# A hand-planned attention and mixer kernel: the steps of its first fifty microseconds in another order, two more q/k groups transposed whole-array

## The chip, the cores and the metric

The kernel runs on one core of one Trainium2 chip. The metric is the device time of one execution in microseconds (us). Three runs of the kernel before gave 184.23, 184.74 and 185.72 us, so the median is 184.74 us.

Engines are named as in the profile: PE is TensorE, ACT is ScalarE, DVE is VectorE, POOL is GpSimd, and SP is SyncE, which here issues nearly all DMAs.

## What is computed

Sigmoid attention for 8 batches of 12 heads, 448 rows and 64 columns each, followed by a token mixer and an output product. In short, from the reference:

```python
scores = scale * np.matmul(q, k.transpose(0, 1, 3, 2)) - np.log(S)
attn = 1.0 / (1.0 + np.exp(-scores))
x = np.matmul(attn, v)            # heads side by side: (8, 448, 768)
wq = x @ w_q                      # (8, 448, 64)
wk = x @ w_k
W_tok = scale * np.einsum('bsd,btd->bst', wq, wk)
mixed = np.einsum('bst,btd->bsd', W_tok, x)
out = np.maximum(mixed, 0.0) @ w_out
```

## The kernel before

The work is cut into 24 groups of four heads (three groups to a batch). A group has seven slices of keys. For each slice PE makes the scores (step S: four 64-column matmuls that use the four quarters of the array at once), ACT takes the sigmoid (line 332, one instruction of 128x896 for each S), and PE multiplies by v (step P, accumulating over the seven slices). After a group's seventh P the result is copied out of the accumulator as `xt` (line 356). Over the whole run that makes 168 S, 168 sigmoids and 168 P.

Before its S steps a group needs q and k transposed. They come in as f32 by DMA, are cast to bf16 on POOL or DVE (lines 212 and 222), and are then transposed in one of these ways, chosen by a letter in the plan:

- `q` with `k` or `j`: on PE in 64x64 pieces, 28 matmuls for q and 28 for k, then one copy of both by DVE (line 301; for group 1 two copies at line 293).
- `a` with `b`: on PE with the whole array, seven 128x128 matmuls each, into a single accumulator bank, each followed by its own DVE copy (line 280).
- `r` with `s` and `z`, or `c` with `d`: on DVE by 32x32 stream transposes (lines 265, 252 and 272), without PE.

The mixer's steps are x (transposing `xt` into `xn`: `x` by 28 pieces of 64x64, `X` by seven whole-array matmuls), W (the products with w_q and w_k, whole-array in this part), N, U and M (the mixer itself), and O (half an output chunk; whole-array in this part; `o` means that ACT copies the finished chunk out, `O` that DVE does). E and F are matmuls of zeros.

**What sets the order.** Nothing is scheduled by the compiler. A string `PLAN` of 669 letters is walked from left to right, and each letter issues one step on all the engines that it uses. Every engine runs its own instructions strictly in that order. A second string, `BANKS`, gives each step in turn its part of the accumulator memory (digits are pairs of banks, letters are single banks): a step waits until the step that had this part before has been read out. So S steps wait for earlier sigmoids through `BANKS`, and whether a copy runs on DVE or ACT is a matter of upper or lower case (`P` or `p` at a group's seventh slice).

Loads go through a ring of six f32 buffers in the order of the string `ORDER`. SP issues a load only when the buffer's former content has been cast, and SP is a queue too, so a late cast holds up all loads behind it. `BEHIND` makes single loads wait for a numbered matmul, and `HELD` does the same for three stores. `1` casts the next load of a short list on DVE (v of group 0, k of group 2). `D` sends finished output tiles on their way if there are any.

In the words below, S8 is the eighth S and "sigmoid 8" its sigmoid; a stretch of whole-array work is a run of steps that use PE as one 128-wide array, between steps that use its quarters.

Of the kernel before, what the change touches and what calls it, by code (L numbers as in the profile page):

```python
# [17 lines left out]
def kernel(  # L18
# [29 lines left out]
    def pool(name, bufs, **kw):  # L48
# [15 lines left out]
    pairs = [banks[:, 2 * n : 2 * n + 2] for n in range(4)]  # L64
    pairs16 = [banks16[:, 2 * n : 2 * n + 2] for n in range(4)]
    BANKS = (
        "abcd0123200233111020302312031203101031021g2012020120h1g21320"
        "132123103103213012302g01h20h1g2031a32102312g12h1201321gh0210"
        "12h01210321g201321g2h01gh201g20132cd302c302302131e301230ef31"
        "0ef3102102c302d320d320123cd20gh120g102310g102hg102312gh10210"  # L70
        "ef130210ef1302120120320312321031021021321a310320321320120123"
        "020210320120c3210210312"
    )
    given = list("".join(BANKS))
    held = set()
# [54 lines left out]
    def xt(u, j):  # L130
# [5 lines left out]


    PLAN = (
        "SSFKESSES1EEqESDD1DESjPPppSpDpPDSSSqS1kSpPPSqSpSkSDPPSPSxSxr"
        "sSWwDDDDSSwzDPpSPppSpPSrSwSwWsSPpXSPNpSpPPSUSqSzMSSkpSpPpSMS"  # L140
        "ppPSSxSxMScPpSdPSpppSSPwWwrWSSXWDWSSosOSNPpPSpppzPSSOOSxSrPP"
        "ppSUSsppzPSoSOSoSoSppMpSPPPPSSWOWWWScSdxWODSMDWSOSxCOSMppScP"
        "DppSPPDSodDoSpxPDPDSCPrPSpDSPOOSNSsSOoDzOOSUSXcSPdpPSSpPPSPo"
        "OWSMSwowWMSSOwWCScpppSxpdpSpPSOoMSPPcDSPPpSpSPOoNSSSdDOoDOOp"
        "xDSPpPxSPpPDSuwcWwdSSMWOoSMSDwwOOSDxpPSPrPSmPpPDooNDSDSosoOz"
        "oSDDSxOOSUDpSDPPPDSPpcDSPoDODSSSodOoOSPMpSPPPSPPSwWwoScMSdOw"
        "wSSWOONSPMPcpSPPPPSSOodXSOSxoSoxSOppSpcUPSPpPSoOSdSxOOSPPPmp"
        "pPSPoSoMmOSOLScllLSLLSDodODSONxOPSpcpdpDPSPSPoOSoSOSOoSUSoSO"
        "SpPPpp1SoSOpSPOSOyppPMpPpplMlmlxlLlxOoONooUoOMmooOmooOoOOOOO"
        "oOOOOooOo"  # L150
    )
    PLAN = "".join(PLAN)
    KIND = ["a"] + [t for t in PLAN if t in "qacr"]
# [364 lines left out]

    opened = []
    stores, o_tiles = [], [0]  # L520
    HELD = {(5, 1, 1): 3040, (5, 2, 0): 3168, (5, 2, 1): 3168}

    def flush(n=None):

# [45 lines left out]
    def out_pair(act, tail):  # L570
# [36 lines left out]
        def store():  # L607
            for x in range(2):
                cols = slice(x * NB, (x + 1) * NB)
                if len(us) == 1:  # L610
                    behind_product(
                        (nc.scalar if ends and x else nc.sync).dma_start(
                            out=out[2 * w + us[0]].rearrange("(p i) d -> p i d", i=NI)[:, k : k + 5 : 4, cols], in_=o[HALF[x]],
                        ), HELD.get((2 * w + us[0], k, x), 0),
                    )
# [6 lines left out]

        stores.append((o_tiles[0] - 1, max(HELD.get((2 * w + us[0], k, x), 0) for x in range(2)), store))
        if tail or late:
# [74 lines left out]
    for _ in range(31):  # L699
# [2 lines left out]

    ORDER = (
# [5 lines left out]
    )  # L709
    BEHIND = {("q", 23): (2280, 2280), ("v", 23): (2816, 2530)}  # L710
    BY = {"s": [], "v": []}
    for x in ORDER.split():
        if x[0] == ".":
# [10 lines left out]
    def pump_loads():  # L724
        while len(loaded) < len(ORDER):
            nm, n = ORDER[len(loaded)]
            if len(ring) >= 6 and ring[-6] not in cast:
                break
            emit, m = BEHIND.get((nm, n), (0, 0))
            if emit >= len(products):  # L730
# [204 lines left out]
```

## Time and profile before

| | before |
|---|---|
| median of three runs | 184.74 us |
| profiled execution, its time | 184.71 us |
| its span, first to last instruction | 182.8 us |
| outside the span (184.71 - 182.8) | 1.9 us |
| sigmoids | 168, busy 141.1 us |
| stores and loads | 48.51 MB, mean 265 GB/s |

The profile comes from one execution, which has a time of its own beside its span; the two differ by what lies around the instructions. The page gives for each engine the share of the span in which it was busy. Busy ends of matmuls are modelled and include the time until the last column is out, so PE can read as busy while no new matmul starts; where this matters the start times of successive matmuls are used instead. A group's row gives its count, total, mean length and the idle time in front of it with what ended that. In the timeline, rows with a count merge instructions of the same kind, and the bracket behind a row is the idle time ahead of it.

### The profile page before, as it was taken

How to read it: one execution, taken by the hardware profiler on the slowest of the kernel's cores; microseconds unless marked ns; L12 is line 12 of the kernel's file. 1: busy time of each engine (PE TensorE's matmuls, PEld its weight loads, DVE VectorE, ACT ScalarE, POOL GpSimd, SP SyncE). 2: the span in 40 equal slices, each digit the busy share in tenths (PEclk: the TensorE clock that was granted, in tenths of full speed). 3: DMA queues.
4: the chain of work that ended last, by engine and by line, in shares of the span. 5: the costliest groups of instructions: out<-in, count | busy, mean ns of one | idle time of the engine just before them, and what ended most of it. 6: DMA issues, size and time to landing. Idle time of an engine off the chain costs nothing.

```text
span 182.8 us, 8404 instructions
## 1 busy us (share of the span) xinstructions
PE 170.4 (93%) x3617; PEld 112.8 (62%) x3618; DVE 134.3 (73%) x205; ACT 159.4 (87%) x207; POOL 116.8 (64%) x156
## 2 busy tenths in 40 slices
PE   7887789899999999999999999999999999999980
PEld 7644435545564555565556556556788798899960
DVE  2545699988998898988858887689786885694220
ACT  4699999999999999999998999899989979966230
POOL 1336886999589999699999927999999500000000
PEclk9999999999999999999999999999999999999997
DMA  5999999969999677999999999997589343433775
GB/s 174 371 382 274 329 382 398 364 212 279 351 402 331 219 295 207 353 285 349 396 232 327 349 307 292 359 359 250 193 255 252 106 96 87 95 90 93 176 181 164
DMA packets 24261, 48.51 MB, mean 265 GB/s; under 512 B 3872, under 2 KB 16416, under 8 KB 24224
## 3 DMA queue, kind: packets, MB, share of 16 engines
q1 hardware_dynamic: 24000, 47.69, 79.4%
q8 instruction: 28, 0.46, 1.0%
q10 hardware_dynamic: 224, 0.30, 0.7%
q14 instruction: 9, 0.07, 0.1%
HBM read 35.78 MB, written 11.01 MB: 256 GB/s over the span
## 4 chain that ended last, share of the span: by engine, by line
PE 76%; ACT 12%; DMA 3%; POOL 3%; issue 2%; DVE 1%; POOLq 0%; ACTq 0%
PE banks L121 72%; ACT at L332 12%; PE banks L124 4%; DMA ld<-in_v_dram 3%; POOL v L222 1%; POOL qk L212 1%; POOL qk L173 1%; POOL wout L755 0%; DVE xn L385 0%; ACT qk L806 0%; DVE ld L558 0%; ACT ld L558 0%; DVE zeros L691 0%; DVE zeros L690 0%; POOLq L222 0%
## 5 line engine op out<-in xcount | busy, mean ns | idle before, releaser
L332 ACT ACTIVATE at<-banks 128x896 bf16<-128x896 f32 x168 | 141.1, 943 | 5.4 <-PE banks L121 4.8
L121 PE MATMUL banks<-wout,mx 64*64 64x384 bf16 (+2 forms) x816 | 65.4, 324 | 0.0
L121 PE MATMUL banks<-qk 64*64 64x448 bf16 x672 | 60.7, 360 | 3.8 <-ACT at L332 3.0
L212 POOL CAST qk<-ld 128x896 bf16<-128x896 f32 x38 | 44.7, 1191 | 8.2 <-issue 5.6
L121 PEld LDWEIGHTS <-mx 64*64 64x64 bf16 (+2 forms) x816 | 39.2, 105 | 16.2 <-issue 6.0
L121 PE MATMUL banks<-at,v 64*64 64x448 bf16 x672 | 46.5, 350 | 0.8 <-ACT at L332 0.4
L121 PEld LDWEIGHTS <-qk 64*64 64x64 bf16 x672 | 26.5, 105 | 24.8 <-issue 17.8
L356 DVE CAST xt<-banks 128x896 bf16<-128x896 f32 x23 | 25.0, 1086 | 7.6 <-PE banks L121 5.7
L121 PEld LDWEIGHTS <-v 64*64 64x64 bf16 x672 | 22.9, 106 | 6.8 <-issue 1.7
L470 DVE TENSOR_SCALAR mx<-banks 128x896 bf16<-128x896 f32 (+1 forms) x21 | 19.9, 956 | 4.9 <-PE banks L121 4.2
L222 POOL CAST v<-ld 128x896 bf16<-128x896 f32 x22 | 20.3, 930 | 2.9 <-DMA ld<-in_v_dram 2.7
L272 DVE STREAM_TRANSPOSE qk<-qk 128x448 f32<-128x448 f32 x26 | 16.0, 630 | 0.1
L385 DVE COPY xn<-banks 128x896 bf16<-128x896 bf16 x21 | 13.1, 624 | 3.6 <-PE banks L124 2.6
L252 DVE STREAM_TRANSPOSE qk<-qk 32x448 f32<-32x448 f32 x24 | 15.3, 636 | 0.6
L170 POOL COPY qk<-qk 32x448 uint32<-32x448 uint32 x26 | 14.4, 554 | 1.6
L173 POOL COPY qk<-swap 32x448 uint32<-32x448 uint32 x26 | 14.4, 554 | 1.5
L121 PE MATMUL banks<-xt,wqk 64*64 64x448 bf16 (+1 forms) x84 | 13.8, 353 | 0.2 <-ACT at L332 0.2
L651 DVE COPY o<-banks 128x384 f32<-128x384 f32 x17 | 9.4, 554 | 3.4 <-PE banks L121 3.0
L124 PEld LDWEIGHTS <-xt 64*64 64x64 bf16 (+1 forms) x588 | 9.8, 108 | 3.0 <-issue 1.5
L124 PE MATMUL banks<-ident,xt 64*64 64x64 bf16 (+1 forms) x588 | 10.4, 194 | 0.2
L121 PE MATMUL banks<-wqk,tmp 64*64 64x448 bf16 (+3 forms) x72 | 8.5, 291 | 0.0
L121 PE MATMUL banks<-wq,tmp 64*64 64x448 bf16 (+2 forms) x72 | 8.4, 292 | 0.0
(67 smaller groups left out, 135.3 us busy)
## 6 DMA issues: line engine op xcount, KB each, us to landing
ld<-in_q_dram SPq DMA_DIRECT2D x24, 448.0 KB, 6.2
ld<-in_v_dram SPq DMA_DIRECT2D x24, 448.0 KB, 5.9
ld<-in_k_dram SPq DMA_DIRECT2D x23, 448.0 KB, 5.9
out_dram<-o SPq DMA_DIRECT2D x38, 192.0 KB, 4.7
out_dram<-ld SPq DMA_DIRECT2D x14, 192.0 KB, 2.8
ld<-in_moe_w_out_dram SPq DMA_DIRECT2D x6, 384.0 KB, 4.6
wout<-wout SPq DMA_DIRECT2D x6, 192.0 KB, 6.0
out_dram<-o SPq DMA_DIRECT2D x4, 96.0 KB, 1.9
```

What stands on the lines that cost most here:

```text
L121: products.append(nc.tensor.matmul(*args, **kw))
L124: products.append(nc.tensor.transpose(*args, **kw))
L170: eng.tensor_copy(out=w[lo, 1], in_=w[hi, 0])
L173: eng.tensor_copy(out=w[hi, 0], in_=z[lo])
L212: COPY[e](out=f[:, :, "qk".index(nm)].rearrange("p e i d y -> p e y i d"), in_=ld.pop((nm, n)).rearrange("p (y i e d) -> p e y i d", y=2, ...
L222: COPY[e](out=t16.rearrange("p i b d -> p b i d"), in_=ld.pop((nm, n)).rearrange("p b (i d) -> p b i d", i=NI),)
L252: nc.vector.transpose(out=qk[n][other : other + 32, h].rearrange("p t i n -> p (t i n)").bitcast(F32), in_=w[own : own + 32, 1 - h],)
L272: nc.vector.transpose(out=qk[n][:, t].rearrange("p t i n -> p (t i n)").bitcast(F32), in_=w)
L332: nc.scalar.activation(dst, src, ACTF.Sigmoid, bias=attn_bias, scale=attn_scale)
L356: COPY[eng](out=xt(u, j), in_=ps)
L385: COPY[eng](out=xn, in_=ps)
L470: nc.vector.tensor_scalar(dst, ps, moe_scale, 0.0, ALU.mult, ALU.max)
```

## The change

The strings `PLAN` and `BANKS` are others, `HELD` has other matmul numbers, and `BEHIND` loses its entry for q of group 23 and has other numbers for v of group 23. `ORDER` is only broken into lines at other places: the loads stand in the same order. The last 340 letters of `PLAN` are the same in both. Of the two strings one line each is shown, at the place where `PLAN` begins:

```diff
     PLAN = (
-        "SSFKESSES1EEqESDD1DESjPPppSpDpPDSSSqS1kSpPPSqSpSkSDPPSPSxSxr"
...
+        "SSFKESSES1EEDDqESDSjSSDS1pDPPpSpSPqpp1kSPpPpSSapSPSSbSxSSXSS"
...
-    HELD = {(5, 1, 1): 3040, (5, 2, 0): 3168, (5, 2, 1): 3168}
+    HELD = {(5, 1, 1): 2916, (5, 2, 0): 3044, (5, 2, 1): 3044}
...
-    BEHIND = {("q", 23): (2280, 2280), ("v", 23): (2816, 2530)}
+    BEHIND = {("v", 23): (2746, 2404)}
```

Counted over the strings, up to the 340 letters that both share: the number of S, P, W, O, N, U, M, E and x steps is the same. Group 3 goes from `q`,`k` to `a`,`b`; group 4 goes from `r`,`s`,`z` to `a`,`b`. Two of the x steps (of groups 1 and 3) go from `x` to `X`. The `xt` copies of groups 0 and 2 go from DVE to ACT. Two more output chunks are copied by ACT and two fewer by DVE. One pair of S steps shares one sigmoid instruction of 128x1792. The kernel issues 70 matmuls fewer in all. Counted in stretches of whole-array work, there are six before S48 and twenty from there to S97 in the kernel before; in the changed kernel there are nine and eighteen.

On ACT, from its first sigmoid on, one piece of the difference (`at` is the sigmoid's output, `xt` a group's result, `o` an output chunk):

```order
-L332 ACTIVATE at<-banks 128x896 x63
+L332 ACTIVATE at<-banks 128x896 x12
+L356 CAST xt_90<-banks 128x2x7x64
+L332 ACTIVATE at<-banks 128x896 x14
+L356 CAST xt_92<-banks 128x2x7x64
+L332 ACTIVATE at<-banks 128x896 x37
 L651 COPY o<-banks 128x384
```

The 63 sigmoids that stood in a row now have two copies of 128x896 among them, after the twelfth and after the twenty-sixth.

On DVE, the rows from the first cast of a whole load to the copies of x, in the kernel before (`q_233` is q of group 1, `v_286` v of group 0, `k_413` k of group 2, `qk_453` the cast q and k of group 4):

```order
L222 CAST q_233<-ld_102 128x2x7x64
L293 COPY qk<-banks 128x2x448
L222 CAST v_286<-ld_104 128x2x7x64
L293 COPY qk<-banks 128x2x448
L356 CAST xt_90<-banks 128x2x7x64
L222 CAST k_413<-ld_105 128x2x7x64
L301 COPY qk<-banks 128x2x2x448 x2
L356 CAST xt_91<-banks 128x2x7x64
L385 COPY xn<-banks 128x896 x2
L265 STREAM_TRANSPOSE qk<-qk_453 128x448 x2
L252 STREAM_TRANSPOSE qk<-qk_453 32x448 x4
```

And the same place of the changed kernel:

```order
L222 CAST q_233<-ld_102 128x2x7x64
L293 COPY qk<-banks 128x2x448 x2
L222 CAST v_335<-ld_104 128x2x7x64
L222 CAST k_413<-ld_105 128x2x7x64
L301 COPY qk<-banks 128x2x2x448
L280 COPY qk<-banks 128x7x2x64
L356 CAST xt_91<-banks 128x2x7x64
L280 COPY qk<-banks 128x7x2x64
L385 COPY xn<-banks 128x896 x2
L280 COPY qk<-banks 128x7x2x64 x2
```

The cast of k of group 2 no longer stands behind a copy of `xt`, both copies of group 1's q and k come ahead of the cast of v, and six stream transposes have given way to copies at line 280.

On PE, around S71 of the kernel before (`wqk` with `xt` is a W step, `wout` with `mx` an O step, `qk` an S step, the `wq`,`tmp` matmul the end of an M step):

```order
L121 MATMUL banks<-wq_99,tmp 64x448
L121 LDWEIGHTS wqk_84
L121 MATMUL banks<-xt_92,wqk_84 128x448
L121 LDWEIGHTS qk
L121 MATMUL banks<-qk 64x448
...
L121 LDWEIGHTS mx
L121 MATMUL banks<-wout_83,mx 128x384
```

And of the changed kernel:

```order
L121 MATMUL banks<-wq_99,tmp 64x448
L121 LDWEIGHTS qk
L121 MATMUL banks<-qk 64x448
...
L121 LDWEIGHTS wqk_84
L121 MATMUL banks<-xt_92,wqk_84 128x448
L121 LDWEIGHTS mx
L121 MATMUL banks<-wout_83,mx 128x384
```

The W step now stands right ahead of the O step, so that the two make one stretch of whole-array work. At S62 and S63 two O steps come together in the same way.

More of the change, by code (lines that the diff above doesn't have):

```diff
@@ L66 @@
     BANKS = (
[L67 to L72, printed above, removed]
+        "abcd230010132022211321302312301g010h1230e31ef03e10033e01f320"
+        "32023102310310g213201302g01h20h1g2031a32102312g121h021301gh0"
+        "21012h01210321g201321gh201gh201g20132cd302c302302131f301230e"
+        "f310ef3102102c302d320d320123cd20gh120g102310g102hg102312gh10"
+        "210ef130210ef1302120120320312321031021021321a310320321320120"
+        "123020210320120c3210213212"
     )
@@ L138 @@
     PLAN = (
-        "SSFKESSES1EEqESDD1DESjPPppSpDpPDSSSqS1kSpPPSqSpSkSDPPSPSxSxr"
[L140 to L150, printed above, removed]
+        "SSFKESSES1EEDDqESDSjSSDS1pDPPpSpSPqpp1kSPpPpSSapSPSSbSxSSXSS"
+        "awwDSSbpPrSppPppwDWSESwWXDSPNSPDPpSpSDspPUSSzSMSqkPDSPSPMPSp"
+        "pPSSXxSSSMpppcSdPppSPSwDwDrWwSSXWWSsCSOOSDDNPzpSpppSpSPoOSxS"
+        "rppPPSUSsPpPzSOSOSDSOoSPMPSpPPSPPSWowwcSSdxOWWSCMSWODSxoSMpP"
+        "SPPpSpcPSOdoSPxrpSpPpSPPDSOoNSTSszOoOOSUSXScppSPpppSdSPOOWSM"
+        "SDwWoWMSSwWOScPpCpSxPppSDdPDSOoMSPPcDSPPpSpSPOoNSSSdDOoDOOpx"
+        "DSPpPxSPpPDSuwcWwdSSMWOoSMSDwwOOSDxpPSPrPSmPpPDooNDSDSosoOzo"
+        "SDDSxOOSUDpSDPPPDSPpcDSPoDODSSSodOoOSPMpSPPPSPPSwWwoScMSdOww"
+        "SSWOONSPMPcpSPPPPSSOodXSOSxoSoxSOppSpcUPSPpPSoOSdSxOOSPPPmpp"
+        "PSPoSoMmOSOLScllLSLLSDodODSONxOPSpcpdpDPSPSPoOSoSOSOoSUSoSOS"
+        "pPPpp1SoSOpSPOSOyppPMpPpplMlmlxlLlxOoONooUoOMmooOmooOoOOOOOo"
+        "OOOOooOo"
     )
```

8 rows, old and new, of the table ORDER are left out of this document.

## The prediction

> **What bounds the kernel now.** I read the page first, then the busy time by stretch, then the chain of waits in order of time, and last the timelines of ACT, PE and DVE over the first 60 us.
>
> ```profile
> span 182.8 us, 8404 instructions
> PE 170.4 (93%) x3617; PEld 112.8 (62%) x3618; DVE 134.3 (73%) x205; ACT 159.4 (87%) x207; POOL 116.8 (64%) x156
> PE 76%; ACT 12%; DMA 3%; POOL 3%; issue 2%; DVE 1%; POOLq 0%; ACTq 0%
> ```
>
> The page says PE, with ACT close behind. A mean over the span hides that they take turns, so I cut the span into stretches. The columns are: stretch, its length, busy time of PE, weight loads, DVE, ACT and POOL with instruction counts, the granted TensorE clock, the DMA share and GB/s.
>
> ```profile
> 7.00:44.00 37.00, 31.36 (x792) 17.70 (x793) 28.24 (x41) 36.67 (x46) 27.71 (x33) 1.00 0.95 333
> 44.00:50.00 6.00, 5.93 (x89) 3.10 (x92) 5.83 (x11) 6.00 (x8) 3.89 (x6) 1.00 1.01 338
> 50.00:130.00 80.00, 80.00 (x1372) 45.54 (x1368) 67.76 (x101) 76.87 (x101) 69.96 (x91) 1.00 0.91 310
> 130.00:160.00 30.00, 30.00 (x854) 25.75 (x850) 21.47 (x31) 28.33 (x36) 13.53 (x20) 1.00 0.56 153
> 160.00:178.00 18.00, 17.58 (x486) 15.84 (x477) 8.68 (x17) 8.45 (x16) 0.00 (x0) 1.00 0.55 134
> ```
>
> From 7 to 44 us ACT is full (36.67 of 37) and PE is not (31.36, and that includes the tails of its matmuls). From 50 us on PE is full. The granted clock is 1.00 in all of them, so the clock has no term here. There are two stages: until about 44 us the sigmoids set the pace and PE follows; after it PE works off its queue to the end. The chain of waits agrees, with one exception in between:
>
> ```profile
> 34.64 0.93 ACT at L332
> ...
> 35.61 1.78 PE banks L121 x28
> ...
> 41.53 5.77 DMA ld<-in_v_dram
> ...
> 47.42 0.94 POOL v L222
> ...
> 48.41 3.48 PE banks L121 x50
> ```
>
> ACT until 35.57, then a load of v (group 6) and its cast on POOL, then PE from 48.41 almost alone. The detour looks important, since it covers 11 us. The timeline of ACT says that it is not:
>
> ```profile
> 6.71 5.78 ACT L332 ACTIVATE at<-banks 128x896 bf16<-128x896 f32 x7 [0.69 <-PE banks L121]
> 12.72 37.67 ACT L332 ACTIVATE at<-banks 128x896 bf16<-128x896 f32 x46 [0.23 <-PE banks L121]
> ```
>
> 46 sigmoids, the eighth to the fifty-third, stand without a break in 37.67 us, 0.82 us each; neighbours overlap by a little, and where nothing disturbs them the step from one start to the next is 0.80 us (rows for it follow). PE can issue S no sooner than the banks are read out, and until S53 that is this rhythm. The chain takes the v load because it was the last of several things to come, not because much was waiting for it.
>
> From this follows the rule of my sum. Both plans have done the same counts of P, W, O, M, N, U and x when they reach S48, and from there on the same letters remain. After S48 PE is full. So the change of the time is: how much later or earlier PE reaches S48, plus what the remaining PE work loses or gains. What is only shuffled ahead of S48 is worth nothing unless it moves the sigmoids.
>
> **Part 1: two `xt` copies on ACT.** They stand inside the row of sigmoids. A copy of 128x896 from the accumulator to bf16 on ACT has a near relative, the relu of the same size, and one smaller copy:
>
> ```profile
> 106.65 0.94 ACT L468 ACTIVATE mx<-banks 128x896 bf16<-128x896 f32 x1
> 107.45 0.51 ACT L651 COPY o<-banks 128x384 f32<-128x384 f32 x1
> 107.87 0.92 ACT L332 ACTIVATE at<-banks 128x896 bf16<-128x896 f32 x1
> ```
>
> From start to start the relu takes 0.80 us, so two copies cost ACT 1.60 us, all of it on the path, since ACT has 0.33 us of idle time in 37 us. The same copy took DVE 1.09 us (its row follows), so ACT is the quicker engine for it, but the full one. The Trainium skill's page ScalarE: Activation LUTs, section Rules for kernel authors, puts simple elementwise work on VectorE rather than ScalarE; in this trace the instruction alone says the contrary (0.94 against 1.09 us), and the idle time says the same as the page.
>
> Against the 1.60 stands what ACT lost here before. Sigmoid 1 starts at 6.71, the eighth at 12.72: 6.01 us where seven steps of 0.80 would be 5.60. The missing 0.41 us is S8 waiting for k of group 1:
>
> ```profile
> 10.92 0.38 PE L121 MATMUL banks<-qk 64*64 64x448 bf16 x4 [0.24 <-ACT at L332]
> 11.11 0.41 PE L124 MATMUL banks<-ident,k 64*64 64x64 bf16 x26
> 11.61 0.62 DVE L293 COPY qk<-banks 128x896 bf16<-128x896 bf16 x1 [0.90 <-PE banks L124]
> ```
>
> S7 (10.92) waits for its bank pair until sigmoid 5 is out, and the transposes of k stand behind S7 in PE's queue. In the changed `BANKS` S7 has the pair of S4, one sigmoid (0.80 us) sooner. Then the copy of k ends about 11.4 instead of 12.24 and S8 is in time: 0.41 us regained. Sum of part 1: 1.60 - 0.41 = +1.2 us at S48. Lower bound: no loss is left at all. The fifty-third sigmoid ends at 12.72 + 37.67 = 50.39 and, 0.92 us long, began at 49.47; 52 steps of 0.80 us from 6.71 would have brought it at 48.31, so 1.16 us were lost in all, and 1.60 - 1.16 = +0.4. Upper bound: nothing regained, and one more stop of the length of a DVE copy (0.62), +2.2.
>
> **Part 2: DVE and the loads.** DVE loses two copies of `xt`, a joint copy of q and k and six stream transposes and gains four copies; it is not on the path, and I cost its relief at nothing, since ACT is full whatever DVE does. One thing does come sooner:
>
> ```profile
> 13.36 1.09 DVE L356 CAST xt<-banks 128x896 bf16<-128x896 f32 x1 [1.13 <-PE banks L121]
> 14.37 0.63 DVE L222 CAST k<-ld 128x896 bf16<-128x896 f32 x1
> 15.02 0.37 SPq L667 DMA_DIRECT2D ld<-in_moe_w_q_dram  x1
> ```
>
> The cast of k of group 2 stood behind the wait and the copy of `xt` (1.13 + 1.09 us), and SP issued the next load at 15.02, right after that cast. Now it stands behind neither, so the whole stream of loads can run up to 2.2 us ahead. While sigmoids set the pace that is worth nothing by itself. Its one visible use is the v of group 6:
>
> ```profile
> 47.96 0.38 PE L124 MATMUL banks<-ident,wqk 64*64 64x64 bf16 x14
> 48.41 0.76 PE L121 MATMUL banks<-at,v 64*64 64x448 bf16 x12
> ```
>
> PE's modelled end before it is 48.34, and 14 short transposes need about 0.1 of the 0.45 us between the starts, so 0.07 to 0.36 us were lost. PE comes later by part 1 and the load sooner, so the wait goes: -0.2 us.
>
> **Part 3: PE.** Group 4 leaves DVE for PE, group 3 and two x steps go from quarters to the whole array:
>
> ```profile
> 29.58 0.56 PE L124 MATMUL banks<-ident,xt 128*128 128x128 bf16 x7
> 30.07 0.38 PE L121 MATMUL banks<-qk 64*64 64x448 bf16 x4
> 33.07 0.41 PE L124 MATMUL banks<-ident,q 64*64 64x64 bf16 x28 [0.16 <-DVE xt L356]
> 33.30 0.38 PE L121 MATMUL banks<-qk 64*64 64x448 bf16 x4
> ```
>
> Seven whole-array transposes hold PE for 0.49 us until the next step, 28 quarter pieces for 0.23. So two for group 4 cost 0.98, two for group 3 cost 0.52 more and two x steps 0.52 more: 2.0 us more PE work before S48. It is covered by the time in which PE waits for sigmoids: 5.6 us of 37 even by the modelled ends. I cost it at nothing. If that cover were gone it would be the 2.0 us.
>
> After S48 the stretches of whole-array work go from twenty to eighteen. What a stretch costs by itself shows where S and O steps alternate, against where two of each come together:
>
> ```profile
> 49.95 0.55 PE L121 MATMUL banks<-qk 64*64 64x448 bf16 x8
> 50.44 1.14 PE L121 MATMUL banks<-wout,mx 128*128 128x384 bf16 x6
> 51.51 0.38 PE L121 MATMUL banks<-qk 64*64 64x448 bf16 x4
> ...
> 55.56 0.38 PE L121 MATMUL banks<-qk 64*64 64x448 bf16 x4
> 55.88 0.66 PE L121 MATMUL banks<-wout,mx 128*128 128x384 bf16 x3
> 56.47 0.38 PE L121 MATMUL banks<-qk 64*64 64x448 bf16 x4
> 56.78 0.66 PE L121 MATMUL banks<-wout,mx 128*128 128x384 bf16 x3
> 57.38 0.38 PE L121 MATMUL banks<-qk 64*64 64x448 bf16 x4
> ```
>
> The same work takes 1.56 us together (49.95 to 51.51) and 1.82 us apart (55.56 to 57.38), 0.26 us for a stretch. Two fewer, where PE is full: -0.5 us. If other waits fill the place it is 0. The Trainium skill's page TensorEngine Tiling (Array Packing), section Key Properties, says that changing the tiling mode drains the TensorE; the 0.26 us agree. By that rule the three more stretches ahead of S48 speak against this change, and that is the slower rival below.
>
> **Part 4: the rest.** Two more chunk copies on ACT after S60 (0.42 us each by the rows 107.45 and 107.87) fall where ACT has 3.1 us of idle time in 80 us and PE is full: 0, and at most +0.8. The joint sigmoid of 1792 does as many elements in one instruction: 0. The load of q of group 23 and the three stores begin sooner, in the last third:
>
> ```profile
> 129.90 0.33 SPq L190 DMA_DIRECT2D ld<-in_q_dram  x1
> 138.50 2.31 POOL L212 CAST qk<-ld 128x896 bf16<-128x896 f32 x2
> ```
>
> The cast comes 8.6 us after the issue because POOL has other casts to do, so the load is not waited for: 0, with a few tenths either way for transfers that meet others.
>
> **Sum.** +1.2 - 0.2 - 0.5 = +0.5 us. The profiled execution took 184.71 us (span 182.8), 0.03 under the median of 184.74, so the forecast is 185.2 us for both. All bounds together give 184.71 + 0.4 - 0.36 - 0.5 = 184.3 and 184.71 + 2.2 + 0.8 = 187.7.
>
> **The rivals.**
> - *Slower: PE has no room ahead of S48.* The transposes of x and of group 4 share one bank (x1, then q4, k4, x2, each waiting for the DVE copy before it), and S29 needs the last copy of group 4. If this chain reaches S29 late, or the 2.0 us of added PE work stand ahead of S steps that ACT waits for, they come on top: 185.2 + 2.0 = 187.2 us. It decides once the copy of k4 ends after sigmoid 28 begins. Against it: by the rows above a member takes 0.49 us on PE and 0.62 on DVE, so the three that S29 needs take 3.3 us; in `PLAN` x1 stands right behind S21, and from there to S29 are eight sigmoids, 6.4 us.
> - *Faster: the loads were the bound.* Then the detour in the chain counts in full, and what the stream gains is the gain: 184.71 - 2.2 - 0.5 = 182.0 us. For it: 11 us of the chain. Against it: sigmoids without a break from 12.72 to 50.39.
> - *The copies are nearly free.* The bounds of part 1 at their low end, 184.3 us. For it: the 1.16 us lost before are of the size of the copies. Against it: a third of them is a wait that I found removed, and nothing says so of the rest.
>
> **Chances.** A measurement of this kernel tells about 1% (1.8 us) from no change. Forecast 0.55, nearly free 0.17, slower rival 0.17, faster rival 0.11. The forecast and the free case lie within 1% (182.9 to 186.6), less 0.02 for the upper end of the forecast: faster 0.11, same 0.70, slower 0.19. The range of 183.9 to 187.0 us leaves out the faster rival and about half of the slower one.
>
> **What would show it.** Right: ACT busy without a break from 7 to 45 us, sigmoid 53 ending about 1.2 us after 50.39; sigmoid 8 starting near 12.3; fewer idle microseconds on PE before 44 us and none more after; P of group 6 not released by POOL. Part 1 is wrong if sigmoid 53 comes no later than before, or more than 2.2 us later; part 3 is wrong if an S before S48 waits for a copy at line 280. The forecast as a whole is wrong if PE shows waits of more than a microsecond after 50 us, since then PE's queue does not set the end.

## The result, and the profile after

| | before | after |
|---|---|---|
| median (12 runs each, same chip) | 184.25 us | 186.19 us |
| lowest and highest | 182.95, 186.33 | 185.20, 188.28 |
| profiled execution, its time | 184.71 us | 186.62 us |
| its span | 182.8 us | 184.7 us |

The ratio is 1.0098, with a 95% interval of 1.0073 to 1.0122: slower by about 1%, at the edge of what I had called no change. The forecast was 185.2 us with a range of 183.9 to 187.0. A few single runs of this case belong to a second, slower state and the ratios leave them out, so a ratio is not quite the quotient of its two medians.

The head of the page of the changed kernel: PE and ACT are as full as they were, and DVE has 5.6 us less to do.

```profile
span 184.7 us, 8259 instructions
PE 170.9 (93%) x3547; PEld 114.5 (62%) x3548; DVE 128.7 (70%) x198; ACT 161.3 (87%) x210; POOL 116.4 (63%) x156
PE 76%; ACT 13%; DVE 4%; DMA 3%; issue 2%; SPq 0%; ACTq 0%; DVEq 0%
```

The busy time by stretch of the changed kernel, with the columns of the same view in the prediction:

```profile
7.00:44.00 37.00, 30.57 (x693) 18.02 (x694) 22.19 (x34) 35.71 (x46) 27.95 (x35) 1.00 0.98 343
44.00:50.00 6.00, 5.85 (x81) 2.99 (x78) 5.92 (x10) 6.00 (x9) 4.03 (x5) 1.00 1.01 352
50.00:130.00 80.00, 79.71 (x1389) 45.98 (x1381) 66.59 (x100) 77.05 (x100) 67.69 (x88) 1.00 0.92 301
130.00:160.00 30.00, 29.62 (x790) 25.22 (x791) 21.11 (x30) 27.79 (x34) 15.39 (x23) 1.00 0.53 155
178.00:185.00 7.00, 2.32 (x32) 1.28 (x24) 1.27 (x3) 1.12 (x3) 0.00 (x0) 0.99 0.68 182
```

Two things stand out. ACT, which had lost 0.33 us from 7 to 44 us, now loses 1.29. And PE is busy for 2.32 us after 178 us, where before it had nothing left to do. The timeline of ACT in the changed kernel shows where the first comes from (start, length, instruction, count, idle time ahead and its releaser):

```profile
6.12 1.73 ACT L332 ACTIVATE at<-banks 128x896 bf16<-128x896 f32 x2 [0.48 <-PE banks L121]
9.01 8.21 ACT L332 ACTIVATE at<-banks 128x896 bf16<-128x896 f32 x10 [1.16 <-PE banks L121]
16.99 1.02 ACT L356 CAST xt<-banks 128x896 bf16<-128x896 f32 x1
17.77 11.59 ACT L332 ACTIVATE at<-banks 128x896 bf16<-128x896 f32 x14
29.17 0.99 ACT L356 CAST xt<-banks 128x896 bf16<-128x896 f32 x1
30.03 30.51 ACT L332 ACTIVATE at<-banks 128x896 bf16<-128x896 f32 x37
```

There are two sigmoids, then a gap of 1.16 us, and from the third on no break any more: 10, 14 and 37 sigmoids in rows with the two copies between them. The copies take 0.78 and 0.86 us from their start to the next sigmoid. The gap is the news. The same place with PE and DVE:

```profile
7.30 0.29 DVE L816 CAST k<-ld 128x256 bf16<-128x256 f32 x1 [1.35 <-DMA ld<-in_k_dram]
7.65 0.51 PE L124 MATMUL banks<-ident,k 64*64 64x64 bf16 x16 [1.26 <-DVE k L816]
8.03 0.49 DVE L802 COPY qk<-banks 128x256 bf16<-128x256 bf16 x2 [0.44 <-PE banks L124]
8.38 0.38 PE L121 MATMUL banks<-zeros 64*64 64x448 bf16 x4 [0.22 <-DVE qk L802]
8.57 0.57 PE L121 MATMUL banks<-qk 64*64 64x448 bf16 x8
```

The zeros step and S3 (8.38, 8.57) have bank pairs that the last parts of group 0's k were transposed into, and so they wait for DVE's copies of these parts, which wait for a load of k. Before, S3 had the pair of S1: it stood behind the same transposes in PE's queue, but not behind DVE's copies of them, of which it needs nothing.

I follow the rest by one number for each place: how much later a sigmoid starts than the same sigmoid of the kernel before. In this execution the first sigmoid is 0.59 us earlier, the seventh 0.70 later, the 37th 1.93 (38.40 against 36.47), the 60th 1.90, the 96th 2.02, the 144th 2.06 and the last 2.74 (161.00 against 158.26). So nearly all is there by 37 us and stays. The last step of 0.69 us is a stop of PE in the middle of an O step, whose releaser the trace does not show:

```profile
136.95 0.39 PE L121 MATMUL banks<-qk 64*64 64x448 bf16 x4
137.14 0.36 PE L121 MATMUL banks<-wout,mx 64*64 64x384 bf16 x3
137.88 1.13 PE L121 MATMUL banks<-wout,mx 64*64 64x384 bf16 x21 [0.38 <-issue]
```

That the two spans differ by 1.9 and not by 2.7 us has its cause at the very end. In the profile of before, the last store was issued at 178.42 and took 0.96 us to issue, and the span ended 4.4 us after 178.42; in the profile of after these are 181.10, 0.49 and 3.6 us.

```profile
178.42 0.96 SPq L562 DMA_DIRECT2D out_dram<-ld  x1
```

```profile
181.10 0.49 SPq L562 DMA_DIRECT2D out_dram<-ld  x1
```

This is no work of the change. In the profiles of the experiments below the same stretch takes 3.6 to 3.8 us, in variants of both kernels, and only in e12, a variant of the kernel before, 4.4. The profile of before was one with a slow end.

### The profile page after: what moved, and what is told of

It reads as the page before. It is cut to its first block, busy times and chain, and to the rows that moved or that the text cites. A ratio compares the mean times of both kernels' runs of the same rounds, so it can differ in the third digit from the quotient of the medians.

```text
span 184.7 us, 8259 instructions
## 1 busy us (share of the span) xinstructions
PE 170.9 (93%) x3547; PEld 114.5 (62%) x3548; DVE 128.7 (70%) x198; ACT 161.3 (87%) x210; POOL 116.4 (63%) x156
## 4 chain that ended last, share of the span: by engine, by line
PE 76%; ACT 13%; DVE 4%; DMA 3%; issue 2%; SPq 0%; ACTq 0%; DVEq 0%
PE banks L121 70%; ACT at L332 12%; PE banks L124 6%; DMA ld<-in_k_dram 3%; DVE xn L385 1%; DVE qk L252 1%; ACT xt L356 0%; DVE qk L265 0%; DVE qk L280 0%; DVE tmp L463 0%; DVE xt L356 0%; SPq L687 0%; SPq L688 0%; DVE ld L558 0%; ACT ld L558 0%
## 5 line engine op out<-in xcount | busy, mean ns | idle before, releaser
L332 ACT ACTIVATE at<-banks 128x896 bf16<-128x896 f32 (+1 forms) x167 | 141.2, 957 | 6.7 <-PE banks L121 6.0
L121 PE MATMUL banks<-qk 64*64 64x448 bf16 x672 | 61.5, 358 | 5.7 <-ACT at L332 4.3
L121 PEld LDWEIGHTS <-mx 64*64 64x64 bf16 (+2 forms) x816 | 39.7, 105 | 16.6 <-issue 6.2
L212 POOL CAST qk<-ld 128x896 bf16<-128x896 f32 x36 | 42.3, 1192 | 11.0 <-issue 8.0
L121 PE MATMUL banks<-at,v 64*64 64x448 bf16 x672 | 47.4, 350 | 0.0
L356 DVE CAST xt<-banks 128x896 bf16<-128x896 f32 x21 | 22.7, 1082 | 6.5 <-PE banks L121 4.6
L121 PEld LDWEIGHTS <-v 64*64 64x64 bf16 x672 | 23.7, 106 | 5.1 <-issue 0.4
L252 DVE STREAM_TRANSPOSE qk<-qk 32x448 f32<-32x448 f32 x20 | 12.7, 635 | 0.5
L651 DVE COPY o<-banks 128x384 f32<-128x384 f32 x15 | 8.3, 554 | 3.4 <-PE banks L121 3.0
```

The costliest lines, as they stand in the source:

```text
L121: products.append(nc.tensor.matmul(*args, **kw))
L212: COPY[e](out=f[:, :, "qk".index(nm)].rearrange("p e i d y -> p e y i d"), in_=ld.pop((nm, n)).rearrange("p (y i e d) -> p e y i d", y=2, ...
L252: nc.vector.transpose(out=qk[n][other : other + 32, h].rearrange("p t i n -> p (t i n)").bitcast(F32), in_=w[own : own + 32, 1 - h],)
L332: nc.scalar.activation(dst, src, ACTF.Sigmoid, bias=attn_bias, scale=attn_scale)
L356: COPY[eng](out=xt(u, j), in_=ps)
```

## The experiments

The twelve runs, each timed in five rounds beside the kernel before on the same chip (its medians in the three series: 184.62, 184.58 and 184.91 us). The last three columns are from one profile each: how much later than in the profile of before the 37th, 96th and last sigmoid start, in us. They contain what happened ahead of the first sigmoid, up to which all these plans have the same letters: it starts between 0.59 us earlier (the change) and 0.07 us later (e2) than in the profile of before, 0.21 earlier in e3 and 0.49 in e6. So a difference of half a microsecond between two rows is not resolved by these columns alone; steps from one sigmoid to another inside a profile are free of this.

| run | median | ratio, 95% interval | 37th | 96th | last |
|---|---|---|---|---|---|
| the change | 186.19 | 1.0098 [1.0073, 1.0122] | 1.93 | 2.02 | 2.74 |
| e8, the change again | 185.77 | 1.0086 [1.0052, 1.0120] | 1.44 | 1.53 | 1.92 |
| e1, before, copies on ACT | 186.19 | 1.0095 [1.0060, 1.0130] | 1.87 | 1.75 | 1.75 |
| e2, after, copies on DVE | 188.79 | 1.0230 [1.0188, 1.0272] | 3.57 | 3.76 | 5.46 |
| e3, after, S3 on other pairs | 185.61 | 1.0064 [1.0032, 1.0096] | 1.20 | 1.53 | 2.09 |
| e4, both | 187.93 | 1.0165 [1.0107, 1.0222] | 2.19 | 2.90 | 2.90 |
| e5, e3 with one copy on DVE, k2 cast first | 185.38 | 1.0057 [1.0033, 1.0081] | 0.99 | 1.32 | 1.39 |
| e6, before with the gains | 185.62 | 1.0060 [1.0030, 1.0091] | 0.60 | 0.69 | 0.72 |
| e7, e3, S80 to S84 as before | 185.74 | 1.0072 [1.0041, 1.0103] | 0.92 | 0.98 | 1.22 |
| e9, e7 with copies on DVE, free pairs | 186.47 | 1.0093 [1.0057, 1.0129] | 1.83 | 1.88 | 2.58 |
| e10, e3, instructions displaced | 186.69 | 1.0101 [1.0063, 1.0138] | 1.01 | 1.33 | 2.76 |
| e11, before, two merges | 184.54 | 1.0001 [0.9963, 1.0039] | -0.06 | 0.04 | 0.35 |
| e12, before, k2 cast first | 184.92 | 0.9993 [0.9963, 1.0023] | 0.29 | 0.18 | 0.48 |

**e1: the kernel before with only the two copies on ACT.** In `PLAN` the seventh P of groups 0 and 2 is lower case:

```diff
-        "SSFKESSES1EEqESDD1DESjPPppSpDpPDSSSqS1kSpPPSqSpSkSDPPSPSxSxr"
-        "sSWwDDDDSSwzDPpSPppSpPSrSwSwWsSPpXSPNpSpPPSUSqSzMSSkpSpPpSMS"
+        "SSFKESSES1EEqESDD1DESjPPppSpDppDSSSqS1kSpPPSqSpSkSDPPSPSxSxr"
+        "sSWwDDDDSSwzDPpSPppSppSrSwSwWsSPpXSPNpSpPPSUSqSzMSSkpSpPpSMS"
```

> The kernel before, with only the xt copies of groups 0 and 2 moved from DVE to ACT (two letters of PLAN). Theory A (the row of sigmoids sets the pace until S48, so each copy put into it is paid in full): sigmoid 53 some 1.2 to 1.6 us later than in the kernel before, and the whole 0.9 to 1.6 us slower, ratio 1.005 to 1.009. Theory B (the copies cost nothing, and the changed kernel's loss lies in its other steps): ratio within 0.997 to 1.003 and sigmoid 53 within 0.4 us of where it was.

Sigmoid 13 is 0.80 us later, the 19th 1.17, the 37th 1.87, and 1.75 are left from the 66th to the end. The copies are paid for in full and carried to the end: 0.80 us for the first, and 0.74 for the second (from the 20th to the 27th sigmoid 1.17 goes to 1.91). The 0.37 us between them (from the 14th to the 18th sigmoid) are not theirs. From 17 to 21 us the granted clock fell in this profile, to 0.54 on the mean from 18 to 21 us, and PE was late there; e3, with the same copy on ACT and the clock at 1.00, loses 0.02 us between these sigmoids. The same stretch of e1 and of the kernel before (the clock is the third number from the end):

```profile
18.00:21.00 3.00, 2.91 (x84) 1.96 (x80) 0.27 (x1) 2.93 (x4) 2.46 (x4) 0.54 1.03 370
```

```profile
18.00:21.00 3.00, 2.46 (x68) 1.32 (x61) 1.31 (x2) 3.00 (x5) 2.48 (x4) 1.00 0.92 286
```

So the ratio of 1.0095 is close to that of the change (1.0098), but the two times are not made of the same pieces. Here the Trainium skill's page ScalarE: Activation LUTs, section Rules for kernel authors, which puts relu, add and the like on VectorE, names the better engine, though not by the length of the copy: 0.90 and 1.00 us on ACT here, 1.09 us on DVE in the profile of before.

**e2: the changed kernel with these two copies back on DVE.** The edit is the reverse of e1's, in the changed `PLAN`:

```diff
-...SPqpp1kSPpPp...SppPppwDW...
+...SPqPp1kSPpPp...SppPpPwDW...
```

> The changed kernel, with the xt copies of groups 0 and 2 put back on DVE. Theory A: it gets 1.2 to 1.6 us back, ratio to the kernel before 1.001 to 1.004. Theory B (the other steps are what costs): it stays at 1.008 to 1.011. Theory C (DVE needed the relief: the cast of k of group 2 and the copies of groups 3 and 4 now come late): sigmoids stop for DVE between S13 and S30, and the ratio stays at or above 1.009.

It is not faster but slower than the change, by 1.3%. DVE, PE and ACT of this run around S13:

```profile
16.48 1.09 DVE L356 CAST xt<-banks 128x896 bf16<-128x896 f32 x1 [4.11 <-PE banks L121]
17.49 1.23 DVE L222 CAST k<-ld 128x896 bf16<-128x896 f32 x1
18.77 0.41 PE L124 MATMUL banks<-ident,k 64*64 64x64 bf16 x28 [2.19 <-DVE k L222]
19.01 0.36 PE L121 MATMUL banks<-qk 64*64 64x448 bf16 x4
19.43 0.92 ACT L332 ACTIVATE at<-banks 128x896 bf16<-128x896 f32 x1 [2.48 <-PE banks L121]
```

The copy waits 4.11 us for the last P, and behind it in DVE's queue stands the cast of k of group 2, which PE needs before S13: ACT is idle for 2.48 us. In this order of steps the copy could not stay on DVE. The rule of e1 does not decide here; the queue does.

**e3: the changed kernel, S3 on other pairs.** From the zeros step ahead of S3 on, pairs 1 and 2 are exchanged, so that S3 takes the pair of S1 as before.

```diff
-    "abcd230010132022211321302312301g010h...
+    "abcd230012231011122312301321302g020h...
```

> The changed kernel with the bank pairs 1 and 2 exchanged from the zeros ahead of S3 on, so that S3 waits for sigmoid 1 and no longer for the DVE copy of k's last part. Theory A2 (the late third sigmoid, 2.07 us after the second in the changed kernel's profile, comes from this bank): the step from sigmoid 2 to sigmoid 3 falls to 0.8 to 1.4 us and the whole is 0.3 to 0.8 us shorter than the changed kernel, ratio to before 1.005 to 1.008. Theory B2 (that load landed late by chance and S3 stands behind the transposes of that part in any case): the step follows the landing of the load, and the ratio stays at 1.008 to 1.011.

The gap after sigmoid 2 is gone (12 sigmoids in a row from 6.50 us), and the 37th sigmoid is 1.20 us later than before instead of 1.93:

```profile
6.50 9.98 ACT L332 ACTIVATE at<-banks 128x896 bf16<-128x896 f32 x12 [0.48 <-PE banks L121]
16.29 0.99 ACT L356 CAST xt<-banks 128x896 bf16<-128x896 f32 x1
17.07 11.56 ACT L332 ACTIVATE at<-banks 128x896 bf16<-128x896 f32 x14
28.44 0.99 ACT L356 CAST xt<-banks 128x896 bf16<-128x896 f32 x1
```

Not all of that is the pair. From the transposes of k's last parts to the zeros step it takes 0.35 us in e3, and 0.73 in the change (7.65 to 8.38) as well as in its second profile, e8:

```profile
7.33 0.52 PE L124 MATMUL banks<-ident,k 64*64 64x64 bf16 x16 [0.69 <-DVE k L816]
7.68 0.36 PE L121 MATMUL banks<-zeros 64*64 64x448 bf16 x4
```

So the pair costs S3 about 0.4 us, and what is left of the gap of 1.16 us came with the load of k, which the transposes ahead of S3 need in either kernel. In time e3 is 0.3% less than the change, and the intervals overlap.

**e4: e2 and e3 together** (both diffs above).

> The changed kernel with both: copies back on DVE and the other banks from S3 on. If A and A2 hold the gains add: 1.6 to 2.3 us shorter than the changed kernel, ratio to before 0.997 to 1.002. If only A holds: 1.001 to 1.004. If neither: 1.008 to 1.011.

A stop of 2.88 us from sigmoid 12 to 13 remains, as in e2 (3.49). So it belongs to the copy's place on DVE and not to the pairs. The ratio of 1.0165 lies outside all that I had expected.

**e5: e3 with the copy of group 0 on DVE, and the cast of k of group 2 ahead of it.**

```diff
-...DDqESDSjSSDS1pDPPpSpSPqpp1kSPpPp...
+...DDqESDSjSSDS1pDPPpSpSPq1PpkSPpPp...
```

> The third variant of the bank pairs (as in the run with the pairs of S3 exchanged), with the xt copy of group 0 back on DVE, but the cast of k of group 2 issued ahead of it; the xt copy of group 2 stays on ACT. Theory C (with the copy on DVE it was the cast of k behind the waiting copy that stopped S13): the step from sigmoid 12 to 13 falls from 2.9 to under 1.3 us, the copy's 0.80 us on ACT goes, and at most 0.5 us comes back at S14 or S15, which wait for DVE instead. Sigmoid 37 then starts 0.3 to 0.8 us sooner than with the exchanged pairs alone (0.4 to 0.9 later than before), the time is about 185.2. Rival D (it is DVE's load as a whole that stopped S13, whatever the order): a step of 2 us or more stays between sigmoids 12 and 16, and the time is 186.5 or more.

The step from sigmoid 12 to 13 is 1.43 us instead of 2.88, so it was the cast behind the copy. But it is not under 1.3, and what the copy no longer takes from ACT is lost again: from the 7th to the 19th sigmoid this run loses 0.76 us, e3 0.52. At S13 all four pairs are taken (the results of groups 0 and 1, q and k of group 2, and the last S), so S13 waits for sigmoid 12 in any case (it starts at 16.36 us, sigmoid 12 ends at 16.30), and ACT idles for 0.48 us, which is where e3 puts the copy. ACT's idle time here had not been free time for everything.

**e6: the kernel before with the three gains of the prediction and no copy on ACT** (another pair for S7; the cast of k of group 2 ahead of the copy; two stretches fewer at S62/S63 and S71). Pairs 0 and 3 are exchanged from S7 on, and the letters are:

```diff
-...ESjPPppSpDpPDSSSqS1kS...PSoSOSoSoSppMp...xWODSMDWSOSx...
+...ESjPPppSpDp1PDSSSqSkS...PSoSOSSooSppMp...xWODSMDSWOSx...
```

> The kernel before with only the three gains of the prediction and no copy on ACT: S7 takes the pair that a zero step has just left, the cast of k of group 2 goes ahead of the xt copy of group 0, and at S62/S63 and S71 two stretches of whole-array work fewer. Theory A (the terms of the prediction): sigmoid 8 0.4 us sooner, sigmoid 54 another 0.2 us sooner, and from S62 to S74 another 0.5 us, kept to the end: -1.1 us, ratio 0.994, about 183.5. Theory B (PE's queue after S48 is held by the sigmoids' bank releases as often as by its own work, so that fewer stretches are filled by other waits): the first two gains of 0.6 us stand, at S74 nothing more has been gained: ratio 0.997. Theory C (PE is full from 50 us and what is gained ahead of it is lost in the queue): nothing at S142, ratio 1.000.

It is slower, by 0.6%, and none of the theories had that. (The profile is of the quickest of its executions, 184.47 us, and so does not show all of it.) S8 is not regained: from the first to the eighth sigmoid it is 5.97 us against 6.01, because in this order four P steps, which wait for the cast of v, stand ahead of S8 too. Between sigmoids 13 and 19 it loses 1.1 us by two stops of PE that no engine released; e12 shows the second of them. From S60 to S74 it loses 0.15 us instead of gaining 0.5.

**e7: e3 with S80 to S84 as before** (the chunk copies at S72 and S80 on DVE again, S82 and S83 with one sigmoid each).

```diff
-...SWODSxoSMpP...SPPDSOoNSTSszOoOOSUS...
+...SWODSxOSMpP...SPPDSOONSSSszOoOOSUS...
```

> The changed kernel with the pairs of S3 exchanged and, of the later part, the two additional output chunks copied by DVE again and S82 and S83 with a sigmoid each. Theory A (these two edits, put at 0 in the prediction, cost about 0.4 us between S80 and S84): the start of sigmoid 84 to 96 is 0.4 us sooner than with the exchanged pairs alone, the time about 0.4 us less. Rival B (the 0.4 us come from the order of other steps there): no difference over 0.1 us at S84 to S96.

From the 72nd to the 84th sigmoid e3 falls back by 0.32 us and e7 not at all (1.12 to 1.44, and 0.84 to 0.84). But the changed kernel itself falls back by only 0.06 us there, in both its profiles (1.85 to 1.91, and 1.36 to 1.42), and e2 does too; 0.32 us is what e3, e4, e5 and e10 lose, the runs that have both the exchanged pairs and these edits. So the two edits cost about 0.3 us together with the exchanged pairs and next to nothing in the changed kernel. The medians (185.61 and 185.74) do not resolve it.

**e8: the changed kernel once more**, for a second profile.

> The changed kernel as it is, a second profile. Theory A (PE's stop at 137.1 us, which no releaser explains, belongs to one execution and not to the program): no stop in this profile, or one of another length, and the last sigmoid 2.0 us later than before instead of 2.7; the median is near 186.2 as it was. Rival B (the stop belongs to this program's place in the instruction stream): the same stop of 0.7 us at the same O step. The wait of S3 for the copies of k's last parts stays in both: sigmoid 3 about 2 us behind sigmoid 2.

Neither is quite right. The stop of PE at the same O step is there again, but shorter (the 146th sigmoid is 0.44 us later than the 144th, 0.69 in the first profile). The gap behind sigmoid 2 is 0.28 us instead of 1.16, since the load of k landed sooner (DVE's cast of it at 6.81 instead of 7.30). How much S3 loses depends on when a load lands.

**e9: e7 with both copies on DVE and the steps around them moved**, so that S13 and S27 have a free pair.

```diff
-...SPqpp1kSPpPpSSapSPSSbSxSSXSS...   ...SbpPrSppPppwDWSESwWXDSPNS...
+...SPq1kPSSSSpPpSPpapSPbSSxSXSS...   ...SbpPrSpSpPpPESwWSwWXDDPNS...
```

> The changed kernel with the pairs of S3 exchanged and S80 to S84 as before, and both xt copies on DVE again, this time with the steps around them moved so that the S behind each has a free pair: S13 takes the pair of S11 and stands ahead of P1.0, and S27 takes the pair of S25 and stands ahead of the P steps of group 2. Theory A (the copies' price is ACT's time and nothing else; where DVE copied them in earlier variants it was the order of banks and steps that lost as much): no step of over 1.1 us between sigmoids 12 and 30, sigmoid 37 1.2 us sooner than in the run with S80 to S84 as before, so -0.3 to +0.1 against before; the time is 184.4 to 184.9, ratio 1.000 to 1.003. Rival B (DVE can't take them in time, in whatever order): the sum of steps between sigmoids 12 and 30 stays within 0.3 us of that run, time about 185.7.

Theory A fails. S13 and S27 are in time, but other steps are late: 1.27 us at sigmoids 18 and 20, 1.92 at 30, since the P steps of group 1 now wait for the copy (0.42 us at 17.76), and S20 and S30 stand behind other waits. The time, 186.47 us, lies above what either theory had. In four orders of steps with a copy on DVE none was measurably better than with it on ACT. That no such order exists isn't shown.

**e10: e3 with PE's instructions displaced by 32.**

```diff
-    for _ in range(31):
-        mm(pairs[3][:, 0, 0 : 132], zeros[:, 0:P], zeros[:, 0 : 132], start=True, stop=True)
+    for _ in range(47):
+        mm(pairs[3][:, 0, 0 : 87], zeros[:, 0:P], zeros[:, 0 : 87], start=True, stop=True)
```

> The changed kernel with the pairs of S3 exchanged, and 47 warming matmuls of 87 columns at the start in place of 31 of 132 (the same columns in all, 32 instructions more on PE ahead of everything). Theory A (PE stops at 137 us because the next block of its instructions comes late, and the place is set by the count of instructions ahead of it): the stop, if it shows, stands 16 matmuls earlier in the program than the fourth matmul of the O step where all profiles of the changed kernel have it, or it is gone because a slower step stands there. Rival B (the place belongs to that O step, by its data or banks): a stop of 0.1 to 0.7 us ahead of the fourth matmul of the same O step as before. The time is that of the run with the exchanged pairs, 185.6, within 0.5.

The stop moved. PE of this run:

```profile
135.62 0.38 PE L121 MATMUL banks<-at,v 64*64 64x448 bf16 x3
137.14 0.72 PE L121 MATMUL banks<-at,v 64*64 64x448 bf16 x9 [1.14 <-issue]
137.55 0.51 PE L121 MATMUL banks<-qk 64*64 64x448 bf16 x4
137.74 1.29 PE L121 MATMUL banks<-wout,mx 64*64 64x384 bf16 x24
```

It now stands 9 + 4 + 3 = 16 matmuls ahead of the place where the change, e2 and e3 have it, which are the 32 instructions (a weight load and a matmul each). The other stops of this kind agree: 222 and 350 matmuls stand ahead of the two of e6, 351 ahead of that of e12, 2398 ahead of that of the change, e2 and e3, and 2399 ahead of the one here (a trace can lack a record). These places lie 128 and 2048 = 16 x 128 matmuls apart, so they are multiples of 256 instructions. The place is set by the count of instructions ahead of it, and not by the data or the banks of a step. The stop is longer too (1.49 us from start to next start), and the last sigmoid is 2.76 us late. The time of 186.69 us is 1.1 above that of e3, where I had expected no more than 0.5. The DMA view of the same run has one packet of the instruction queue, 16 KB, in the window from 134.6 to 135.8 us and none from there to 138.2:

```profile
q8 instruction: 1, 0.02, 5.2%
```

PE goes on after that packet's window has closed. In all five profiles that I compared (the change, e2, e3, e6, e10) the stop ends 1.2 to 1.6 us after the end of the last such packet. I read it as PE having run out of instructions; that the packet is what ended the stop is inferred from the times, since no event records it.

**e11: the kernel before with only the two merges.**

```diff
-...PSoSOSoSoSppMp...xWODSMDWSOSx...
+...PSoSOSSooSppMp...xWODSMDSWOSx...
```

> The kernel before with only the two merges: S62 and S63 ahead of both O steps, and W beside O behind S71. Theory A (the prediction's 0.26 us for each stretch): sigmoid 74 and all behind it 0.5 us sooner, ratio 0.997. Theory B (S63 now follows S62 at once and waits for the sigmoid before last to leave its pair, 0.2 us each, and the second merge puts W behind an S that others wait for): sigmoid 74 no sooner, 0 to 0.2 us later than before, ratio 1.000 to 1.001.

Theory B holds: the ratio is 1.0001, and sigmoid 76 is 0.10 us later against the first ones. PE of this run at S62 and S63, behind the step that starts at 56.30:

```profile
56.30 0.38 PE L121 MATMUL banks<-qk 64*64 64x448 bf16 x4
56.91 0.38 PE L121 MATMUL banks<-qk 64*64 64x448 bf16 x4 [0.23 <-ACT at L332]
57.23 1.15 PE L121 MATMUL banks<-wout,mx 128*128 128x384 bf16 x6
58.31 0.38 PE L121 MATMUL banks<-qk 64*64 64x448 bf16 x4
```

Two S and two O take 2.01 us here (56.30 to 58.31), and apart they took 1.82 (in the prediction's rows, 55.56 to 57.38). The stretch is saved, but S63 now comes right behind S62, 0.61 us after it, because it waits for a sigmoid to leave its pair. With an O step between them that wait had been covered.

**e12: the kernel before with only the cast of k of group 2 ahead of the copy.**

```diff
-...ESjPPppSpDpPDSSSqS1kS...
+...ESjPPppSpDp1PDSSSqSkS...
```

> The kernel before with only the cast of k of group 2 issued ahead of the xt copy of group 0. Theory A (the loads run ahead and with them the v of group 6, nothing else changes before S48): sigmoid 54 0.2 us sooner, of which nothing is left at S56 since PE's own work holds the next S; ratio 0.999 to 1.000. Theory B (the two stops of PE at 15 and 20 us seen with the three gains together came from this edit: transfers that run ahead delay PE's instruction blocks): stops of PE of 0.6 us or more between 13 and 21 us again, sigmoid 19 0.7 to 1.1 us later than before, ratio 1.003 to 1.007.

The time is unchanged (ratio 0.9993), as Theory A has it, but not by its mechanism. From the 49th to the 54th sigmoid 0.21 us are gained, since v of group 6 comes sooner, and at the 56th 0.15 are lost again. Yet e11, which leaves that cast where it was and has the letters of the kernel before up to S62, gains 0.20 and loses 0.14 at the same sigmoids, since there too v of group 6 is cast sooner. The cast in the profile of before, and in e11:

```profile
47.42 0.93 POOL L222 CAST v<-ld 128x896 bf16<-128x896 f32 x1 [1.51 <-DMA ld<-in_v_dram]
```

```profile
45.85 0.93 POOL L222 CAST v<-ld 128x896 bf16<-128x896 f32 x1 [0.64 <-PE banks L124]
```

So that load was late in the one execution that gave the profile of before, and this gain is not shown to come from the edit. What the edit does give, a load issued at 12.79 instead of 15.02 us, is used up a few loads later (21.50 against 21.55). PE stops once at 19.74 us, after the same 21 of 28 transposes as in e6, though only for half as long. PE of e12:

```profile
18.73 0.35 PE L124 MATMUL banks<-ident,k 64*64 64x64 bf16 x21
19.74 0.25 PE L124 MATMUL banks<-ident,k 64*64 64x64 bf16 x7 [0.66 <-issue]
```

And of e6:

```profile
18.50 0.35 PE L124 MATMUL banks<-ident,k 64*64 64x64 bf16 x21
20.05 0.25 PE L124 MATMUL banks<-ident,k 64*64 64x64 bf16 x7 [1.20 <-issue]
```

The kernel before runs the same 28 transposes without a stop at 18.73 us, and so do e11 and, at its lower clock, e1, in which the load behind the cast is issued at 12.79 us too. So that the sooner cast brings the stop (Theory B) is not shown. No version among these beats the kernel before.

## Why the prediction came out as it did

The range held the time and the mechanism of the largest term was right. The sum of +0.5 us was too small: by the medians it is 1.9 us. That the time still lay in the range is in part luck. The forecast stood on a median of three runs, 184.74 us, half a microsecond above that of twelve, and both gains that I took off the cost of the copies outside part 1 were not there. Of my signs of being right only one came as written: P of group 6 was not released by POOL. Sigmoid 53 ended 1.7 us later where I had put about 1.2, within the bounds of part 1. ACT had a break, sigmoid 8 started at 13.01 instead of near 12.3, and PE's idle time grew, before 44 us from 5.6 to 6.4 us and from 50 to 160 us from 0.0 to 0.7. By its own steps:

- **Part 1, +1.2 us at S48: the size is right for what it counted, and it left one wait out.** Both copies cost their step on ACT (0.80 and 0.74 us in e1), S8 was in time, and with S3 on other pairs the 37th to 49th sigmoid are 1.20 us late (e3). In the changed kernel they are 1.93 and 1.44 us late in two profiles. The 0.2 to 0.7 us more are the wait of S3: about 0.4 us of it for DVE's copies of k, and in the first profile the rest for a load of k that landed late. The 0.41 us of S8 came back, but S7's other pair alone does not bring them (e6): the changed plan also has S8 ahead of the P steps that wait for the cast of v. I had followed `BANKS` at S7, where it gains, and not at S3. My upper bound of +2.2 had room for "one more stop of the length of a DVE copy", and the wait for DVE's copies is a stop of that kind.
- **Part 2, -0.2 us: the wait belonged to one execution.** P of group 6 waits for nothing in the changed kernel, but neither does it in e11, which has the casts of the kernel before. I had read the term from one profile, in which that load was late, and no run shows that the sooner cast of k removes a wait. It was not worth 0.2 us either: in the changed kernel 1.93 at the 49th sigmoid goes to 1.58 at the 55th and is 1.90 again at the 56th, and e11 and e12 gain 0.20 and lose 0.14 or 0.15 likewise. The wait had cost 0.06 us net; that PE's own work up to S56 holds that sigmoid is what I take from it, and it was not tried by itself.
- **Part 3, the 2.0 us of PE work ahead of S48: 0 is right.** From the third sigmoid on ACT has no gap up to S36, and the steps around group 4's transposes run at ACT's pace.
- **Part 3, -0.5 us for two stretches fewer: mis-sized; it measures 0, at worst +0.1 (e11, where S60 to S74 alone lose 0.16).** The 0.26 us are real as a difference of PE's times, but I applied them where an S waits for banks. My ground was that PE is full from 50 us. It is full by modelled ends, and within that it still waits for a sigmoid here and there: the 0.23 us in e11's rows. "If other waits fill the place it is 0" stood in the text as the other end, and I took the wrong one. The page TensorEngine Tiling (Array Packing) of the Trainium skill, section Key Properties, says that changing the tiling mode drains TensorE; the price of it was in the trace, but the bank wait took its place.
- **Part 4, 0: right within 0.1 us for the changed kernel.** From the 72nd to the 84th sigmoid it falls back by 0.06 us in both profiles. The same chunk copies and joint sigmoid cost 0.3 us with other pairs (e3 against e7), so the 0 was not safe: I had argued the +0.8 away with ACT's idle time of 3.1 us in 80 and had not followed the pairs there.
- **Not in the sum at all: PE's stop at 137 us**, 0.44 and 0.69 us in two profiles. My sign of failure, "waits of more than a microsecond after 50 us", did not appear in the changed kernel; its largest was 0.7.

Together, for the first profile: 1.93 at the 37th sigmoid, +0.1 from there to the 144th, +0.7 at the stop, less 0.8 by the last stores, which were slow in the profile of before, are 1.9 us, the difference of the spans.

Of the rivals, the slower one (PE has no room ahead of S48, 187.2 us) named a time that was off by as much as the forecast, 1.0 us on the other side, and its mechanism did not come: no S of that stretch waited for a copy at line 280. Against the faster one (the loads were the bound) speak e12, where a load is issued 2.2 us sooner, and e11, where v of group 6 is cast 1.57 us sooner: no time is gained in either. A stream of loads that stays ahead to the end was not tried. "The copies are nearly free" is refuted by e1.

## What to carry to other kernels

An engine that is full by its busy time may still be waiting inside it. Before a saving there is priced, ask what the next instruction on that engine needs and when that comes free; if it is a buffer of the other full engine, the saving is a wait of the same size. When a table gives out buffers by turns, every place where a step has got another buffer has to be followed, those at the start too, and not only the one that was meant to gain. A wait that is to be priced should be looked for in a second execution first: a load that was late once is no term of the kernel. And an idle time of 0.5 us that is there because all buffers are taken can be the cheapest place for a copy, even on the engine that sets the pace.

## What the runs showed of the hardware

PE stops in the middle of a step, with no releaser, for up to 1.7 us from one start to the next (e2), and it does so at a place that is fixed by the count of instructions ahead of it: displacing 32 instructions moved the stop by exactly 16 matmuls (e10), and the stops listed under e10 lie a multiple of 128 matmuls with their weight loads, 256 instructions, apart (222, 350 and 2398 matmuls, give or take a record). A 16 KB packet of an instruction queue ends 1.2 to 1.6 us before PE goes on. The page of the changed kernel lists 27 such packets, one for every 260 or so of PE's 7,095 matmuls and weight loads:

```profile
q8 instruction: 27, 0.44, 1.0%
```

The length varies from run to run (0.69 and 0.44 us for the same program), and most packets come early enough: the profile of before has no such stop. What decides when a packet is asked for stays open. So a change that only shifts the number of instructions can move the time of a later, untouched part by some tenths of a microsecond. Up to the 144th sigmoid the change was 2.06 us late, and a third of that came on top by such a stop in a part where the letters of both plans are the same.

The granted clock can fall inside a run as well: in e1 to 0.54 on the mean from 18 to 21 us, where the kernel before, e11 and e12 had 1.00, and the sigmoids lost 0.37 us around there. What brought it is open.
